# Reordering the hand-over from the mode mix to the output units, and storing the last row block in two halves

## The chip, the cores and the metric

The kernel runs on one core of one Trainium2 chip. The metric is the device time of one execution in microseconds. The profile is one execution taken by the hardware profiler; its span runs from the first to the last instruction of the program.

## What is computed

The input x has 8 batches of 3264 rows of 192 values. The first part is a causal convolution with 7 taps, with softmax weights for each of 8 heads of 24 columns. The second part is a spectral layer on its result:

```
c = conv7(x)                              # (8, 3264, 192)
X = rfft(c, axis=1)[:, :64]               # 64 modes
Y = X * (w_r + 1j*w_i)                    # a 192 x 192 product for each mode
y = irfft(Y, n=3264, axis=1)
u = c + y
out = u + maximum(u @ w_ch, 0)
```

The kernel writes the product as u @ W = c W + G (Y W), where W is w_ch and G is the inverse transform restricted to 64 modes (128 real rows). So each block of output is: c W, plus G times the "second-stage weights" zw = Y W, clamped at zero, plus G times zy = Y, plus c.

## The kernel before

**Work units.** Rows are cut into 27 windows of 122 rows. A unit (h, w, k) is window w for two batches, 4h + 2k and 4h + 2k + 1, as a [128, 384] block in one PSUM bank. There are 108 units; `seq` holds their order, in which the two units k = 0 and 1 of one (h, w) follow each other, so units 0 to 5 are three windows of h = 0, unit 6 is (1, w, 0) and unit 7 is (1, w, 1). `wq` is the list of (h, w).

**What one unit does.**
- c W on TensorE: transposed convolution results (`cTs`) times W, four matmuls of 192 columns (`ab_full` at L546 on the full array).
- z = G zw, one matmul of 384 columns (`gz`, L538), then the clamp on ScalarE (`relu`, L578).
- the y product G zy, one matmul of 384 columns onto the clamped bank (`gy`, L538).
- the add of c on VectorE into the tile t (`finish_unit`, L608); after the second unit of a (h, w) one DMA on SP's queue stores the [128, 4, 192] block (L618).

**Second-stage weights.** `zw_mm(h, k, banks)` makes zw for one pair of batches with four matmuls of 192 columns (L524). With two banks VectorE copies one half (L528) and ScalarE the other (L529); with one bank VectorE copies all 384 columns (L531). Units with k = 0 of h = 0 need zw(0,0), those with k = 1 need zw(0,1); unit 6 needs zw(1,0), unit 7 needs zw(1,1).

**Order.** Engines take their instructions in the order in which the program issues them (`manual_schedule`); there is no scheduler. Before the first zw stands the mode mix in 16 groups (`mix`, L468), whose weights come by DMA. After the last group the result is scaled (`ymix`, L477), transposed (`mix_t`, L503) and copied to `yeT` (VectorE L505, ScalarE L506). While TensorE waits for the mode weights, c W of five units is made ahead (`prefill`), and `keep_warm` issues products of the identity matrix with itself, whose results are not used. Then comes the hand-over that the change edits, and then the steady loop (`for j in range(NF, N + 6)`).

**Steady loop.** It works on half arrays: a product over 128 rows is done as two products over 64 rows each, on row tile 0 and row tile 1, which run beside each other. In step j, the half 0 of z and c W of unit j runs beside half 1 of unit j - 2 (`z_ops`, L556), then the clamp of unit j - 2, then half 0 of the y product of unit j - 4 beside half 1 of unit j - 5 (`y_ops`, L573), and the add of unit j - 5. Two halves write one bank, so the second half waits for a "word": an empty instruction on POOL behind the last product of the first half (L590, in `run_pair`).

**Banks.** There are eight PSUM banks: three in pool `pza`, four in `pt`, one in `py`; `bank(n)` says which pool unit n draws from. A new unit's bank is one whose former unit has been added.

Of the kernel before, what the change touches and what calls it, by code (L numbers as in the profile page):

```python
# [12 lines left out]
F32 = mybir.dt.float32  # L13
BF16 = mybir.dt.bfloat16
# [4 lines left out]
def kernel(  # L19
# [9 lines left out]
    nc = tc.nc  # L29
    B, S, D = x.shape  # L30
# [5 lines left out]
    P = 128  # L36
    WIN = 122
# [50 lines left out]
    ident = constp.tile([P, P], BF16, tag="ident")  # L88
# [66 lines left out]
    for g in range(4):  # L155
        i0 = OV if g == 0 else 0
# [247 lines left out]
    for p in range(4):  # L404
        k = 0
# [88 lines left out]
    def mix_t(g, ymix):  # L494
        zt = mixed[0]
        et = zt[:, 256:512].bitcast(BF16)[:, 0:2 * P].rearrange("p (t k) -> p t k", t=2)
        ets = [et[:, 0, :], et[:, 1, :]]
        q = 16 * (g // 2)
        if g == NGRP - 1:

            ets[1] = zwps[1][:, 0:P // 2].bitcast(BF16)
        for t in range(2):
            nc.tensor.transpose(ets[t], ymix[:, 64 * t:64 * t + P], ident[:])  # L503
        if g == NGRP - 1:
            nc.vector.tensor_copy(out=yeT[:, 0, :, q:q + 16], in_=ets[0].rearrange("p (q b) -> p b q", b=B))  # L505
            nc.scalar.copy(out=yeT[:, 1, :, q:q + 16], in_=ets[1].rearrange("p (q b) -> p b q", b=B))  # L506
        else:
            nc.vector.tensor_copy(out=yeT[:, :, :, q:q + 16],
                                  in_=et.rearrange("p t (q b) -> p t b q", b=B))
# [8 lines left out]
    def zw_mm(h, k, banks):  # L518
        for i in range(2):
            b = 4 * h + 2 * k + i  # L520
            zp = banks[i % len(banks)]
            o = zp[:, D * i:D * i + D] if len(banks) == 1 else zp[:, 0:D]
            for e, wn in ((0, win0), (1, win1)):
                nc.tensor.matmul(o, yeT[:, e, b, :], wn[:, :],  # L524
                                 start=(e == 0), stop=(e == 1), skip_group_check=True)
        zt = zwip.tile([P, 2 * D], BF16, tag=f"zw{h}{k}", name="zw")
        if len(banks) == 2:
            nc.vector.tensor_copy(out=zt[:, 0:D], in_=banks[0][:, 0:D])  # L528
            nc.scalar.copy(out=zt[:, D:2 * D], in_=banks[1][:, 0:D])  # L529
        else:  # L530
            nc.vector.tensor_copy(out=zt[:], in_=banks[0][:, 0:2 * D])  # L531
        b = 4 * h + 2 * k
        zwi[(h, 0, k)] = zt[:]
        zwi[(h, 1, k)] = zy[:, b:b + 2, :].rearrange("p b e -> p (b e)")
# [15 lines left out]
    def z_ops(u, zp, r):  # L550
        h, w, k = u
        lo, hi = 64 * r, 64 * r + 64
        cTp = cTs[2 * h + k]

        def mm(o, lhsT, rhs, start, stop):
            return nc.tensor.matmul(o, lhsT, rhs, start=start, stop=stop, skip_group_check=True,  # L556
                                    tile_position=(lo, 0))

        ops = [lambda: mm(zp[:, 0:2 * D], gst[lo:hi, WIN * w:WIN * w + P], zwi[(h, 0, k)][lo:hi, :],
                          r == 0, False)]  # L560
        for i in range(2):
            c0 = WIN * (NWIN * i + w)
            ops.append(lambda i=i, c0=c0: mm(zp[:, D * i:D * i + D], cTp[lo:hi, c0:c0 + P],
                                             win0[lo:hi, :], False, False))
        c0 = WIN * (2 * NWIN + w)
        ops.append(lambda: mm(zp[:, D * r:D * r + D], cTp[lo:hi, c0:c0 + P],
                              (wB0[0:64, :], win1[64:P, :])[r], False, False))
        return ops

    def y_ops(u, zp, r):  # L570
        h, w, k = u
        lo, hi = 64 * r, 64 * r + 64
        return [lambda: nc.tensor.matmul(zp[:, 0:2 * D], gst[lo:hi, WIN * w:WIN * w + P],  # L573
                                         zwi[(h, 1, k)][lo:hi, :], start=False, stop=(r == 1),
                                         skip_group_check=True, tile_position=(lo, 0))]
# [3 lines left out]

    SYNC = mybir.DependencyInfo(mybir.DependencyClass.Sync, mybir.DependencyReason.DATA)  # L580

    def run_pair(ops0, ops1, behind):


        word = None
        for i in range(max(len(ops0), len(ops1))):
            if i < len(ops0):
                ins = ops0[i]()
                if i == len(ops0) - 1:
                    word = nc.gpsimd.nop()  # L590
                    tc.add_manual_dep(word.ins, ins.ins.name, SYNC, reason="row tile 0 is done")
            if i < len(ops1):
                ins = ops1[i]()
                if i == 0:
                    tc.add_manual_dep(ins.ins, behind.ins.name, SYNC, reason="row tiles on one bank")
        return word

# [3 lines left out]
    def finish_unit(u, zp):  # L603
        h, w, k = u
        if k == 0:
            ts[h] = p3.tile([P, B // 2, D], F32, tag="t", name="t")
        t = ts[h]
        add = nc.vector.tensor_tensor(  # L608
            out=t[:, 2 * k:2 * k + 2, :],
            in0=zp[:, 0:2 * D].rearrange("p (i e) -> p i e", i=2),  # L610
            in1=x_all[:, 4 * h + 2 * k:4 * h + 2 * k + 2, w, :], op=ALU.add)
        if k == 0:
            return
        rows = ((0, 80), (80, LASTVALID)) if w == NWIN - 1 else ((0, P),)
        for r0, r1 in rows:
            dst = bass.AP(tensor=out.tensor, offset=out.offset + (4 * h * S + WIN * w + r0) * D,
                          ap=[[D, r1 - r0], [S * D, B // 2], [1, D]])
            nc.sync.dma_start(out=dst, in_=t[r0:r1, :, :])  # L618


    CH = 7
# [20 lines left out]
    def prefill():  # L642
        zps.append(junk if len(zps) == 2 else bank(len(zps)))
        ab_full(seq[len(zps) - 1], zps[-1])

    def keep_warm(o, n):

        for _ in range(n):
            nc.tensor.matmul(o[:, 0:P], ident[:], ident[:], start=True, stop=True)

    for g in range(NGRP):
        last = g == NGRP - 1
        m = mix(g)
        if g == 6:
            wts0_stack.close()
            cTb = ctx.enter_context(tc.tile_pool(name="stashb", bufs=1)).tile([P, CTW], BF16, tag="cTb")
            nc.vector.memset(cTb[:, NSLOT * WIN:CTW], 0.0)
            cTs[3] = cTb[:, :]
        if g in (0, 1, 2):
            load_weights(g + 7, wp)  # L660
        elif 7 <= g and g + 4 < NGRP:
            load_weights(g + 4, None if g == 10 else wp)
        if not last:
            for _ in range(TPER[g]):
                t_next(2 if g < 6 else 3)
            if gq:
                g_part(gq.pop(0))
            if g == 2:
                load_weights(10, None)

            if g in (10, 11, 14):
                prefill()
            if g == 11:
                junk = bank(2)
        else:
            keep_warm(zwps[0], 4)
        if m is not None:
            mix_t(g, m)
        if g in (12, 13):
            y_back(g - 12)  # L680
        if g in (11, 12, 13):
            keep_warm(junk, 5)
        if g == NGRP - 2:
            zwps += [pt.tile([P, 512], F32, tag="p", name="zwps") for _ in range(2)]
            prefill()
            prefill()
            keep_warm(zwps[0], 6)
# [15 lines left out]
    def gz(n):  # L703
        g_full(seq[n], zps[n], 0)
        relu(zps[n])

    def gy(n):
        g_full(seq[n], zps[n], 1)
        finish_unit(seq[n], zps[n])

    zw_mm(0, 0, zwps[0:2])
    zw_mm(0, 1, zwps[2:3])
    gz(0)
    zw_mm(1, 0, zwps[0:1])
    gz(1)
    gz(2)
    gy(0)
    gz(3)
    gy(1)
    gz(4)  # L720
    zw_mm(1, 1, zwps[1:2])
    gy(2)
    prefill()
    gy(3)
    gz(5)
    N, NF = len(seq), 6
    zword, yword = {}, {}
    for j in range(NF, N + 6):
        o0, o1 = [], []
        if j < N:  # L730
            zps.append(bank(j))
            o0 = z_ops(seq[j], zps[j], 0)
        if NF <= j - 2 < N:
            o1 = z_ops(seq[j - 2], zps[j - 2], 1)
        zword[j] = run_pair(o0, o1, zword.get(j - 2))
        if NF <= j - 2 < N:
            relu(zps[j - 2])
        elif j == NF:
            gy(NF - 2)
            gy(NF - 1)  # L740
        o0, o1 = [], []
        if NF <= j - 4 < N:
            o0 = y_ops(seq[j - 4], zps[j - 4], 0)
        if NF <= j - 5 < N:
            o1 = y_ops(seq[j - 5], zps[j - 5], 1)
        yword[j - 4] = run_pair(o0, o1, yword.get(j - 5))
        if NF <= j - 5 < N:
            finish_unit(seq[j - 5], zps[j - 5])
# [29 lines left out]
```

## Time and profile before

| what | us |
|---|---|
| median of 4 runs | 180.72 |
| lowest and highest run | 179.97 and 182.24 |
| the profiled execution, its own time | 182.24 |
| its span | 180.4 |
| last product of the mode mix starts a burst at | 108.12 |
| first zw product (L524) starts | 109.78 |
| first half product of unit 6 and of unit 7 (L556) | 113.91 and 114.84 |
| last add (L608) ends | 175.35 |

The engine abbreviations are PE for TensorE (PEld its weight loads), DVE for VectorE, ACT for ScalarE, POOL for GpSimd and SP for the engine that issues the stores. A row of the timeline gives the start, the length, the engine, the line, the operation, output and inputs, and how many instructions it covers; a bracket names the idle time before it and what ended that. A matmul's length includes its way through the array, so starts that follow each other closely tell the pace. A row of the windows gives the stretch, its length, the busy time of each engine with the number of instructions, the clock granted to TensorE, the share of the DMA engines and GB/s.

### The profile page before, as it was taken

The page shows a single profiled execution, that of the slowest core. Times are in us where ns is not written, and L with a number is a line of the kernel's source. Part 1 is how long each engine was busy: PE and PEld are TensorE (multiplying, and loading weights), DVE is VectorE, ACT ScalarE, POOL GpSimd, SP SyncE. Part 2 cuts the span into 40 slices and gives each one's busy share as a digit, 9 for nine tenths or more (in the row PEclk, how much of TensorE's full clock was granted, in tenths as well). Part 3 has the DMA queues.
Part 4 walks back from the last instruction along what each step waited for, and adds up shares of the span by engine and source line. Part 5 has one row for each costly group of instructions (what it writes and reads, how often), then busy time and mean ns, then how long its engine had stood idle before and what let it go on. Part 6 is the DMA issues. An engine that isn't in the chain of part 4 may idle for free.

```text
span 180.4 us, 5471 instructions
## 1 busy us (share of the span) xinstructions
PE 147.5 (82%) x2147; PEld 128.8 (71%) x2147; DVE 130.1 (72%) x260; ACT 112.5 (62%) x189; POOL 51.9 (29%) x81
## 2 busy tenths in 40 slices
PE   0377639998898978886877768999999999999960
PEld 0245528877788868775866756799999999999930
DVE  6879985462553446967677524699999999999980
ACT  2358863565656635775766215588888888888840
POOL 7966745549524344441534000000000000000000
PEclk9999996999999999999999999999999999999996
DMA  5999999999999999999999940669999999999995
GB/s 164 178 190 191 192 191 192 191 189 194 190 191 196 202 206 210 204 207 208 205 206 206 208 82 23 213 224 323 353 339 330 370 343 338 358 346 341 313 338 176
DMA packets 65830, 42.02 MB, mean 233 GB/s; under 512 B 29228, under 2 KB 65804, under 8 KB 65804
## 3 DMA queue, kind: packets, MB, share of 16 engines
q0 software_dynamic: 36048, 19.71, 78.7%
q1 hardware_dynamic: 29226, 21.56, 36.0%
q10 hardware_dynamic: 530, 0.39, 0.7%
q8 instruction: 17, 0.28, 0.6%
q14 instruction: 9, 0.07, 0.1%
HBM read 40.19 MB, written 21.01 MB: 339 GB/s over the span
## 4 chain that ended last, share of the span: by engine, by line
PE 55%; DMA 27%; DVE 10%; issue 3%; POOL 2%; ACT 1%; DVEq 0%; POOLq 0%; ACTq 0%
PE z L556 19%; PE z L573 13%; DMA x_all<-in_x_dram 11%; DMA wt<-in_moe_w_i_dram 11%; PE xp L298 7%; PE cp L276 6%; DMA win<-in_moe_w_ch_dram 4%; PE tp L430 3%; DVE x_all L285 3%; PE yp L468 2%; DVE cTa L434 2%; PE tp L310 1%; DVE xs L302 1%; PE z L538 1%; DVE t L608 1%
## 5 line engine op out<-in xcount | busy, mean ns | idle before, releaser
L608 DVE TENSOR_TENSOR t<-z,x_all 128x384 f32<-128x384 f32 x108 | 59.5, 557 | 3.5 <-PE z L573 1.7
L578 ACT ACTIVATE z<-z 128x384 f32<-128x384 f32 x108 | 50.8, 475 | 12.2 <-PE z L556 1.6
L556 PE MATMUL z<-zw,gst 64*128 64x384 bf16 x204 | 46.5, 323 | 0.1
L573 PE MATMUL z<-zy,gst 64*128 64x384 bf16 x204 | 46.2, 323 | 0.2
L556 PE MATMUL z<-win,cTa 64*128 64x192 bf16 x375 | 41.1, 243 | 0.0
L283 ACT CAST x_all<-cp 122x864 bf16<-122x864 f32 (+2 forms) x34 | 28.5, 878 | 16.3 <-PE cp L276 16.3
L556 PEld LDWEIGHTS <-cTa 64*128 64x128 bf16 x450 | 35.1, 94 | 2.8
L276 PE MATMUL cp<-x_all,cband 128*128 128x192 bf16 (+2 forms) x192 | 26.0, 288 | 8.4 <-DVE x_all L285 3.7
L276 PEld LDWEIGHTS <-cband 128*128 128x128 bf16 x192 | 19.6, 109 | 12.4 <-issue 4.7
L285 DVE CAST x_all<-cp 122x768 bf16<-122x768 f32 (+2 forms) x14 | 14.7, 1056 | 13.9 <-PE cp L276 13.5
L61 POOL DMA_DIRECT2D x_all<-in_x_dram x23 | 21.5, 939 | 11.3 <-DMA x_all<-in_x_dram 10.5
L298 PE MATMUL xp<-x_all,fst 122*128 122x192 bf16 (+1 forms) x216 | 22.3, 253 | 0.9 <-DVE x_all L285 0.5
L435 ACT COPY cTa<-tp 128x854 bf16<-128x854 bf16 (+1 forms) x16 | 14.0, 911 | 10.6 <-PE tp L430 10.4
L298 PEld LDWEIGHTS <-fst 122*128 122x128 bf16 (+1 forms) x216 | 18.5, 100 | 2.1 <-DVE x_all L285 0.7
L556 PEld LDWEIGHTS <-gst 64*128 64x128 bf16 x204 | 19.1, 94 | 0.6 <-issue 0.6
L556 PE MATMUL z<-win,cTb 64*128 64x192 bf16 x135 | 19.2, 243 | 0.0
L556 PE MATMUL z<-wB,cTa 64*128 64x192 bf16 x75 | 18.2, 243 | 0.0
L573 PEld LDWEIGHTS <-gst 64*128 64x128 bf16 x204 | 16.2, 93 | 1.0 <-POOLq L590 0.9
L556 PEld LDWEIGHTS <-cTb 64*128 64x128 bf16 x162 | 14.4, 94 | 1.1
L434 DVE COPY cTa<-tp 128x854 bf16<-128x854 bf16 (+1 forms) x17 | 10.6, 621 | 5.4 <-PE tp L430 5.0
L430 PE MATMUL tp<-ident,x_all 122*128 122x122 bf16 x216 | 13.6, 217 | 0.0
L267 POOL DMA_DIRECT2D wt<-in_moe_w_r_dram x14 | 8.6, 613 | 16.7 <-PE yp L468 9.5
(110 smaller groups left out, 176.8 us busy)
## 6 DMA issues: line engine op xcount, KB each, us to landing
out_dram<-t SPq DMA_DIRECT2D x52, 384.0 KB, 3.9
x_all<-in_x_dram POOLq DMA_DIRECT2D x15, 384.0 KB, 11.0
wt<-in_moe_w_r_dram POOLq DMA_DIRECT2D x14, 288.0 KB, 11.0
wt<-in_moe_w_i_dram POOLq DMA_DIRECT2D x14, 288.0 KB, 11.2
x_all<-in_x_dram POOLq DMA_DIRECT2D x7, 480.0 KB, 9.9
fst<-in_moe_w_r_dram POOLq DMA_DIRECT2D x2, 288.0 KB, 10.1
fst<-in_moe_w_i_dram POOLq DMA_DIRECT2D x2, 288.0 KB, 10.7
out_dram<-t SPq DMA_DIRECT2D x2, 240.0 KB, 3.7
```

Of the source, the lines that this page charges most:

```text
L61: nc.gpsimd.dma_start(out=x_all[:, b, c0:c0 + n, :], in_=src)
L276: nc.tensor.matmul(cp[:, j, 0:GRP * n].rearrange("p (w e) -> p w e", w=n), cband[:, h, :], x_all[:, b, w0:w0 + n, GRP * h:GRP * h + GRP], ...
L283: nc.scalar.copy(out=dst, in_=srcv)
L285: nc.vector.tensor_copy(out=dst, in_=srcv)
L298: nc.tensor.matmul(xp[:, 0:D], fst[0:k, c, :], x_all[0:k, b, c, :], start=(u == FIRST[b] and c == w0), stop=(u == LAST[b] and c == w0 + n ...
L430: nc.tensor.transpose(tp[:, WIN * k:WIN * k + WIN], slot_lhsT(p, k0 + k), ident[0:WIN, 0:WIN])
L434: nc.vector.tensor_copy(out=got[0][0], in_=got[0][1])
L435: nc.scalar.copy(out=got[1][0], in_=got[1][1])
L556: return nc.tensor.matmul(o, lhsT, rhs, start=start, stop=stop, skip_group_check=True, tile_position=(lo, 0))
L573: return [lambda: nc.tensor.matmul(zp[:, 0:2 * D], gst[lo:hi, WIN * w:WIN * w + P], zwi[(h, 1, k)][lo:hi, :], start=False, stop=(r == 1), ...
L578: return nc.scalar.activation(out=zp[:, 0:2 * D], in_=zp[:, 0:2 * D], func=ACT.Relu)
L608: add = nc.vector.tensor_tensor(out=t[:, 2 * k:2 * k + 2, :], in0=zp[:, 0:2 * D].rearrange("p (i e) -> p i e", i=2), in1=x_all[:, 4 * h + ...
```

## The change

Five edits, four of them at the hand-over.

1. c W of six units instead of five is made ahead: the third `prefill` in group 14 stands where one bank of `zwps` was reserved, and the `prefill` between the y products is gone. `zwps` now holds one `pt` bank and the `py` bank.
2. The second transpose of the last `mix_t` writes to `zwps[0]`, and `keep_warm` writes to columns 384 to 511 of its bank instead of columns 0 to 127.
3. zw(0,0) is written to the `py` bank and `zwps[0]`; the three later ones use one of these two in turn. The order of z products, clamps and y products becomes 0 2 4 1 3 5 for the clamps, with each zw made when its units need it.
4. The y products of units 3 and 5 are done in halves: half 1 beside half 0 of units 6 and 7, then half 0 alone, which waits for a word of half 1.
5. The last (h, w) of the list stores its first two batches after the unit k = 0 and its last two after k = 1.

```diff
@@ mix_t
-            ets[1] = zwps[1][:, 0:P // 2].bitcast(BF16)
+            ets[1] = zwps[0][:, 0:P // 2].bitcast(BF16)
@@ run_pair
-    def run_pair(ops0, ops1, behind):
-        word = None
+    def run_pair(ops0, ops1, behind1, behind0=None, want=(0,)):
+        words = [None, None]
         for i in range(max(len(ops0), len(ops1))):
...
+            for n, (ops, behind) in enumerate(((ops0, behind0), (ops1, behind1))):
+                if i >= len(ops):
+                    continue
+                ins = ops[i]()
+                if n in want and i == len(ops) - 1:
+                    words[n] = nc.gpsimd.nop()
+                    tc.add_manual_dep(words[n].ins, ins.ins.name, SYNC, reason="the row tile is done")
+                if i == 0 and behind is not None:
                     tc.add_manual_dep(ins.ins, behind.ins.name, SYNC, reason="row tiles on one bank")
-        return word
+        return words[0] if want == (0,) else words
@@ finish_unit
+        split = (h, w) == wq[-1]
-        if k == 0:
+        if k == 0 and not split:
             return
+        i0 = 2 * k if split else 0
+        nb = 2 if split else B // 2
...
-            nc.sync.dma_start(out=dst, in_=t[r0:r1, :, :])
+            nc.sync.dma_start(out=dst, in_=t[r0:r1, i0:i0 + nb, :])
@@ keep_warm
-            nc.tensor.matmul(o[:, 0:P], ident[:], ident[:], start=True, stop=True)
+            nc.tensor.matmul(o[:, 3 * P:4 * P], ident[:], ident[:], start=True, stop=True)
@@ group 14
-            zwps += [pt.tile([P, 512], F32, tag="p", name="zwps") for _ in range(2)]
+            zwps.append(pt.tile([P, 512], F32, tag="p", name="zwps"))
+            prefill()
             prefill()
             prefill()
@@ hand-over
-    zw_mm(0, 0, zwps[0:2])
-    zw_mm(0, 1, zwps[2:3])
+    zy0 = zwps[1]
+    zw_mm(0, 0, [zy0, zwps[0]])
     gz(0)
+    zw_mm(0, 1, [zy0])
+    gz(2)
+    gz(4)
+    gy(0)
     zw_mm(1, 0, zwps[0:1])
     gz(1)
-    gz(2)
-    gy(0)
+    gy(2)
     gz(3)
+    gy(4)
+    zw_mm(1, 1, [zy0])
+    gz(5)
     gy(1)
-    gz(4)
-    zw_mm(1, 1, zwps[1:2])
-    gy(2)
-    prefill()
-    gy(3)
-    gz(5)
@@ loop, steps j = 6 and 7
+        if j - NF < 2:
+            n = (3, 5)[j - NF]
+            o1 = y_ops(seq[n], zps[n], 1)
+            zword[j], word1 = run_pair(o0, o1, None, want=(0, 1))
+            run_pair(y_ops(seq[n], zps[n], 0), [], None, behind0=word1, want=())
+            finish_unit(seq[n], zps[n])
+            continue
         zword[j] = run_pair(o0, o1, zword.get(j - 2))
         if NF <= j - 2 < N:
             relu(zps[j - 2])
-        elif j == NF:
-            gy(NF - 2)
-            gy(NF - 1)
```

More of the change, by code (lines that the diff above doesn't have):

```diff
@@ L580 @@
     SYNC = mybir.DependencyInfo(mybir.DependencyClass.Sync, mybir.DependencyReason.DATA)
-    def run_pair(ops0, ops1, behind):
-        word = None
+    def run_pair(ops0, ops1, behind1, behind0=None, want=(0,)):
+        words = [None, None]
         for i in range(max(len(ops0), len(ops1))):
[L587 to L594, printed above, removed]
+            for n, (ops, behind) in enumerate(((ops0, behind0), (ops1, behind1))):
[6 more added lines that the diff above has]
+                if i == 0 and behind is not None:
                     tc.add_manual_dep(ins.ins, behind.ins.name, SYNC, reason="row tiles on one bank")
-        return word
+        return words[0] if want == (0,) else words
     ts = {}
@@ L605, in finish_unit @@
         if k == 0:
-            ts[h] = p3.tile([P, B // 2, D], F32, tag="t", name="t")
-        t = ts[h]
+            ts[(h, w)] = p3.tile([P, B // 2, D], F32, tag="t", name="t")
+        t = ts[(h, w)]
         add = nc.vector.tensor_tensor(
@@ L611, in finish_unit @@
             in1=x_all[:, 4 * h + 2 * k:4 * h + 2 * k + 2, w, :], op=ALU.add)
-        if k == 0:
+        split = (h, w) == wq[-1]
+        if k == 0 and not split:
             return
+        i0 = 2 * k if split else 0
+        nb = 2 if split else B // 2
         rows = ((0, 80), (80, LASTVALID)) if w == NWIN - 1 else ((0, P),)
         for r0, r1 in rows:
-            dst = bass.AP(tensor=out.tensor, offset=out.offset + (4 * h * S + WIN * w + r0) * D,
-                          ap=[[D, r1 - r0], [S * D, B // 2], [1, D]])
-            nc.sync.dma_start(out=dst, in_=t[r0:r1, :, :])
+            dst = bass.AP(tensor=out.tensor, offset=out.offset + ((4 * h + i0) * S + WIN * w + r0) * D,
+                          ap=[[D, r1 - r0], [S * D, nb], [1, D]])
+            nc.sync.dma_start(out=dst, in_=t[r0:r1, i0:i0 + nb, :])
     CH = 7
```

## The prediction

> **What bounds the kernel now.** I read the busy table, then the chain of waits around the edited code, then the queues of VectorE and of the stores.
>
> ```profile
> PE 147.5 (82%) x2147; PEld 128.8 (71%) x2147; DVE 130.1 (72%) x260; ACT 112.5 (62%) x189; POOL 51.9 (29%) x81
> ...
> PEclk9999996999999999999999999999999999999996
> ...
> L608 DVE TENSOR_TENSOR t<-z,x_all 128x384 f32<-128x384 f32 x108 | 59.5, 557 | 3.5 <-PE z L573 1.7
> ```
>
> The table alone decides nothing. From 117 to 172 us the chain of waits is TensorE only (L556 and L573), a step every 0.572 us, one step per unit; the add at L608 follows each step with a gap of about 15 ns. An add lasts 557 ns, but where adds queue up they start 465 to 475 ns apart, so VectorE is not the bound there, nor ScalarE (clamps start 371 ns apart when queued). The change leaves the steady steps as they are. It can move only two things: when they begin (before: 115.27 us, row tile 0 of unit 8), and what comes after the last add (175.35 us). So the sum has two terms.
>
> The chain of waits through the start (start, length, what):
>
> ```profile
> 109.43 0.30 DVE yeT L505
> 109.73 0.05 issue
> 109.78 0.52 PE zwps L524 x4
> 110.30 0.02 issue
> 110.32 0.33 ACT zw L529
> 110.65 0.04 issue
> 110.69 0.32 PE z L538
> ...
> 112.63 0.33 PE zwps L524 x4
> 112.96 0.16 PE z L538
> 113.12 0.13 PE z L546 x2
> 113.25 0.06 issue
> 113.31 0.56 DVE zw L531
> 113.87 0.04 issue
> 113.91 0.57 PE z L556 x4
> ```
>
> It shows that the start is latency, not TensorE work: copy of yeT, four products for zw, copy, clamp, and at 113.31 the last copy of a zw on VectorE, for which unit 6 waits.
>
> **The change, part by part.** The prices come from the timeline: matmul starts lie 56, 82 and 162 ns apart for 128, 192 and 384 columns; the result is out 219, 246 and 322 ns after the start; PE to VectorE or ScalarE takes 0.04 us more, back to PE 0.05.
>
> *Unit 5's c W ahead.* Four matmuls of L546 (0.33 us, 112.96 to 113.29) leave the start and stand at 106.9, before the wait for the last mode weights, which ends at 108.12; TensorE idles 0.92 us there, so they cost nothing. Gain in TensorE work: 0.33 us, worth time only if TensorE is what is late. The ident products on cols 384:512 of other banks cost nothing.
>
> *Bank of the second transpose.* It now shares bank zwps[0] with the four ident products behind it. In the built order the first of these waits for ScalarE's copy L506. That copy ended at 109.68, so they start at 109.74 instead of 109.22, and the first zw product at 109.74 + 4 x 0.056 = 109.96 instead of 109.78: **+0.18**. The ident matmuls compute nothing needed; they only stand ahead in TensorE's queue.
>
> *Order 0 2 4 1 3 5, zw over two banks.* From 109.96, zw(0,0) goes to two banks and ScalarE's half ends at 110.81, so clamp 0's product starts at 110.86 (before 110.69). Now zw(0,1) runs behind it (111.02 to 111.52), then units 2 and 4. y product 0 needs clamp 0 (111.22 to 111.70): 111.76, before 111.58. zw(1,0) runs 111.92 to 112.41, then z of 1, y of 2, z of 3, y of 4, zw(1,1) 112.90 to 113.39, z of 5, y of 1, to 113.55. No clamp is late in this order: those of 2, 4, 1, 3 are ready 0.05 us or more before their y products.
>
> What is late next is VectorE, which takes adds and zw copies in program order:
>
> ```profile
> 110.65 0.56 DVE L531 CAST zw<-zwps 128x384 bf16<-128x384 f32 x1
> 111.38 0.56 DVE L531 CAST zw<-zwps 128x384 bf16<-128x384 f32 x1 [0.17 <-PE zwps L524]
> 112.38 1.02 DVE L608 TENSOR_TENSOR t<-z,x_all 128x384 f32<-128x384 f32 x2 [0.44 <-PE z L538]
> 113.31 0.55 DVE L531 CAST zw<-zwps 128x384 bf16<-128x384 f32 x1
> 113.78 2.03 DVE L608 TENSOR_TENSOR t<-z,x_all 128x384 f32<-128x384 f32 x4
> ```
>
> Before: three zw copies, two adds, the copy of zw(1,1), four adds. After: zw(0,1) at 111.55, add 0 at 112.18, zw(1,0) at 112.65, adds 2 and 4 at 113.11 and 113.58, and only then **zw(1,1) at 114.04, done 114.60** (before 113.31 and 113.86). Behind it: unit 7's first product, with everything on TensorE queued after that.
>
> *Units 6 and 7 with y halves.* Unit 6 starts at 113.65 (113.55, plus 0.10 for the change from full array to half array, as between unit 5's y product at 114.585 + 0.162 and 114.844); before 113.91. Half 1 of unit 3's y runs beside it, free. Half 0 waits for the word through POOL: in the drain such halves start 0.43 us apart, so 114.1. TensorE then stands until 114.65 for zw(1,1); unit 7 starts there, before 114.84. Half 0 of unit 5's y follows 0.46 us later (word, LDWEIGHTS), 0.16 us long, and unit 8 can start at 114.65 + 0.62 = **115.27**. Before it was 115.27. **Net of the start: 0.0 us.** The 0.33 us taken off TensorE turns into a wait for VectorE.
>
> *One unseen cost.* In the profile add 0 starts at 112.38 though its last wait ended at 111.96: 0.42 us with no cause in the trace. If that start-up belongs to the first add, all of VectorE behind it slides to the copy of zw(1,1) at 114.40 and unit 8 begins 0.36 us later. [...] Below: without the +0.18 and with no POOL delay, -0.3.
>
> *Last row block in two halves.* The half for k=0 is issued at about 174.9 instead of 175.38. One more DMA issue (0.37 us on SP) fits before the second half at 175.38; nothing queues behind it. Whether it helps is read from the stores:
>
> ```profile
> 174.00:175.00 1.00, 0.44 (x3) 0.09 (x1) 1.00 (x3) 0.00 (x0) 0.00 (x0) 1.00 0.96 320
> 175.00:176.00 1.00, 0.00 (x0) 0.00 (x0) 0.35 (x1) 0.00 (x0) 0.00 (x0) 1.00 1.09 371
> 176.00:177.00 1.00, 0.00 (x0) 0.00 (x0) 0.00 (x0) 0.00 (x0) 0.00 (x0) 1.00 1.10 371
> ```
>
> The last column is GB/s. The last four adds start 0.47 us apart, two per 384 KB store, so the last three stores are issued 0.93 to 0.98 us apart; one takes 1.06 us at 371 GB/s. From 174.8 to 177.8 the 16 engines have no hole, and one engine runs on to 179.1 alone with its backlog. [...] By the row they are full, and bytes that arrive earlier only join a queue: 0.0. I take the row. Bounds: -0.5 and +0.1.
>
> **Sum.** 0.0 (start) + 0.0 (end) against the profiled execution: 182.24 us stays 182.2 (span 180.4 stays 180.4). That was the slowest of the four runs; on their median of 180.72 the same sum gives **180.7**.
>
> **The rivals.**
> *VectorE late by its first add.* +0.36, 181.1. For it: the 0.42 us stood before exactly this instruction. Against: no other add shows it.
> *The half store pays and the start gains a little.* -0.5, 180.2. For it: the end is pure DMA from 175.4 on. Against: 371 GB/s without a hole.
> *The clock drops (slower).*
>
> ```profile
> 23.40:26.90 3.50, 1.02 (x10) 0.99 1.60 191
> 26.90:30.30 3.40, 3.40 (x22) 0.51 1.60 191
> ...
> 105.30:108.80 3.50, 2.58 (x46) 1.00 0.15 28
> 108.80:112.20 3.40, 2.90 (x27) 1.00 0.08 20
> ```
>
> A stretch with TensorE 1.02 us busy was followed by 3.4 us at clock 0.51. The change opens holes: 109.4 to 109.7, 110.3 to 110.9, 114.2 to 114.65. If they brought a stretch down to that share, 3.41 us at half speed would cost 1.7 us in the TensorE-bound part: 182.4. It decides from roughly a third busy (1.02 of 3.5 dropped it, 2.17 of 3.4 at 101.9 to 105.3 did not); the holes take 0.9 us from 2.9, so it should hold.
> *The halves don't overlap as written.* If half 1 of each y product ran alone, 0.16 us for unit 5 only: 180.9.
>
> **How the numbers follow.** Chances: no change 0.58, first add late 0.18, half store pays 0.15, clock 0.06, no overlap 0.03. About 1% (1.8 us) is what a measurement of this kernel tells from no change; only the clock case reaches near it, and the runs themselves lie 2.3 us apart. So faster 0.04, same 0.90, slower 0.06. The range: costs from -0.6 to +0.5 us, and as much again for the median of a few such runs: 179.6 to 181.8.
>
> **What would show it.** The first ident product behind the last transposes starts only after L506 ends (or my +0.18 is wrong); zw(1,1)'s copy starts near 114.0 and unit 7's first product directly behind it; add 0 within 0.1 us of its wait; unit 8 near 115.3 (with the stretch before it shifted alike); the DMA near 370 GB/s until about 2.5 us after the last add, with the last store's landing unmoved relative to the last add. The prediction is wrong if unit 8 begins over 0.5 us earlier, if the DMA has holes behind 175, or if the granted clock drops between 109 and 119.

## The result, and the profile after

The changed kernel takes 181.06 us in the median (43 runs), the kernel before 180.87 us (64 runs). The ratio is **1.0014, 95% interval 0.9997 to 1.0031**: no difference that this measurement can tell, as predicted. The ratio is of fast runs alone, without two of the 43 that lay over 1.5% above the fastest, so it isn't the quotient of the medians. The same kernel was measured again later, as one of the experiments, and gave 1.0044 [1.0023, 1.0064], a small slowdown that is clear of its interval; the middle of the two is 1.003, or +0.5 us. The forecast of "no change" held, but not every zero in its sum was a zero.

From the page of the changed kernel, its busy table, the granted clock in 40 slices, and the group of the adds:

```profile
PE 146.9 (81%) x2149; PEld 128.5 (71%) x2149; DVE 129.3 (72%) x260; ACT 112.9 (63%) x189; POOL 51.8 (29%) x81
...
PEclk9999789999999999999999996999999999999996
...
L608 DVE TENSOR_TENSOR t<-z,x_all 128x384 f32<-128x384 f32 x108 | 59.7, 557 | 3.5 <-PE z L573 1.4
```

Totals and adds are nearly as before. The clock row is not: the single 6 in the middle of the span is a slice around 110 us, in the hand-over, where the kernel before had a 9.

Both profiled spans are 180.4 us (own times 182.34 and 182.24), which hides three differences. The table gives the distances between four landmarks; the last add is in both kernels the 101st after unit 6's.

| stretch, us | before | after |
|---|---|---|
| span's start to the start of the last mode-mix product | 108.35 | 106.42 |
| from there to the start of unit 6's add | 9.11 | 10.37 |
| from there to the start of the last add | 57.34 | 57.35 |
| last add's end to the span's end | 5.00 | 5.75 |

The first row depends on when the mode weights arrive; in the 14 profiles of this study it lies between 106.35 and 108.35, also among kernels whose code up to there is the same. So two profiles are compared from the last mode-mix product on, and not by their spans. On that measure the profiled execution lost 1.26 us in the hand-over and 0.75 us at the end.

**The hand-over.** The chain of waits of the changed kernel (start, length, what):

```profile
108.19 0.34 PE zwps L524 x4
108.53 0.02 issue
108.55 0.33 ACT zw L529
108.88 0.04 issue
108.92 0.32 PE z L538
109.25 0.62 PE zwps L524 x4
109.87 0.96 PE z L538 x3
```

Four zw products take 0.34 us at 108.19 and the next four, of the same shape, 0.62 us at 109.25. Where the same hand-over ran at the full clock (the experiment "The hand-over alone" below), both groups took 0.34 us. The windows of the same profile, PE to POOL busy with numbers of instructions, then the granted clock:

```profile
105.70:109.10 3.40, 1.98 (x28) 1.38 (x29) 0.65 (x2) 0.92 (x3) 0.14 (x1) 1.00 0.08 21
109.10:112.50 3.40, 3.40 (x16) 2.14 (x15) 2.03 (x4) 1.84 (x5) 0.00 (x0) 0.50 0.08 19
112.50:115.90 3.40, 3.40 (x45) 2.57 (x45) 2.72 (x6) 1.58 (x4) 0.00 (x0) 0.99 0.19 66
```

The granted clock was 0.50 from 109.1 to 112.5. This is the slower rival of the prediction, in this execution, and one of the signs by which the prediction said it would be wrong. Whether it is the rule is a question for the experiments. The profiled execution was a long one: 182.34 us against the median of 181.06.

**The end.** The issues of the last block's two halves on SP's queue, after:

```profile
174.63 0.53 SPq L621 DMA_DIRECT2D out_dram<-t  x1
...
175.21 0.76 SPq L621 DMA_DIRECT2D out_dram<-t  x1
```

The last add ended at 174.68. The second half was issued 0.53 us later, because SP was still at work on the first. Before, the one store was issued at 175.38, 0.03 us after the last add's end:

```profile
175.38 0.37 SPq L618 DMA_DIRECT2D out_dram<-t  x1
```

### The profile page after: what moved, and what is told of

The parts are those of the page before. It is cut to its first block, busy times and chain, and to the rows that moved or that the text cites. A ratio compares the mean times of both kernels' runs of the same rounds, so it can differ in the third digit from the quotient of the medians.

```text
span 180.4 us, 5477 instructions
## 1 busy us (share of the span) xinstructions
PE 146.9 (81%) x2149; PEld 128.5 (71%) x2149; DVE 129.3 (72%) x260; ACT 112.9 (63%) x189; POOL 51.8 (29%) x81
## 4 chain that ended last, share of the span: by engine, by line
DMA 50%; PE 37%; POOL 7%; issue 2%; DVE 1%; ACT 1%; DVEq 0%; POOLq 0%; ACTq 0%
DMA x_all<-in_x_dram 26%; DMA wt<-in_moe_w_i_dram 24%; PE z L556 19%; PE z L573 14%; POOL x_all L61 4%; PE z L538 2%; PE zwps L524 1%; PE yp L468 1%; DVE t L608 1%; POOL wt L267 1%; POOL x_all L74 1%; POOL x_all L67 0%; POOL x_all L66 0%; DVEq L782 0%; POOL midx L123 0%
## 5 line engine op out<-in xcount | busy, mean ns | idle before, releaser
L573 PE MATMUL z<-zy,gst 64*128 64x384 bf16 x208 | 47.2, 323 | 0.2
L276 PE MATMUL cp<-x_all,cband 128*128 128x192 bf16 (+2 forms) x192 | 25.0, 281 | 7.8 <-DVE x_all L328 5.0
L298 PE MATMUL xp<-x_all,fst 122*128 122x192 bf16 (+1 forms) x216 | 21.4, 246 | 0.9 <-DVE x_all L285 0.5
L298 PEld LDWEIGHTS <-fst 122*128 122x128 bf16 (+1 forms) x216 | 17.7, 98 | 1.9 <-DVE x_all L285 0.7
```

The costliest lines, as they stand in the source:

```text
L276: nc.tensor.matmul(cp[:, j, 0:GRP * n].rearrange("p (w e) -> p w e", w=n), cband[:, h, :], x_all[:, b, w0:w0 + n, GRP * h:GRP * h + GRP], ...
L298: nc.tensor.matmul(xp[:, 0:D], fst[0:k, c, :], x_all[0:k, b, c, :], start=(u == FIRST[b] and c == w0), stop=(u == LAST[b] and c == w0 + n ...
```

## The experiments

Four questions: what does the start cost at full clock; is it VectorE's queue that takes the gain; how often does the clock drop; what does the half store cost? The runs fall into three groups: the first four kernels below, the next four, the last four. Each group has its own runs of the kernel before (medians 180.73, 180.48 and 180.59 us). Stage times are from one profile each; "start" is from the last mode-mix product to unit 6's add (9.11 before), "end" from the last add's end to the span's end (5.00 before). In all kernels the steady part between takes 57.34 or 57.35 us.

### The half store alone

The kernel before, with only the `split` lines of `finish_unit`.

```diff
 # kernel before
+        split = (h, w) == wq[-1]
...
-            nc.sync.dma_start(out=dst, in_=t[r0:r1, :, :])
+            nc.sync.dma_start(out=dst, in_=t[r0:r1, i0:i0 + nb, :])
```

> The kernel before with the store of the last row block in two halves, and nothing else. Theory 1 (the DMA engines have no hole at the end, bytes that arrive earlier only join a queue): 0.0 us, ratio 0.999 to 1.001, time from the end of the last add to the last landing as before, 4.1 us. Theory 2 (the half store pays, as if the engines were idle): -0.5 us, 3.6 us from last add to last landing. Theory 3 (the store before it keeps SP busy, so that the last one is issued late): +0.3 us, the last store is issued 0.3 to 0.5 us behind the end of the last add instead of 0.03.

Measured: 1.0029 [1.0011, 1.0046]; start 9.10, end 5.81. The half store by itself costs about 0.5 us, all of it behind the last add. The last landing comes 4.46 us after the last add's end (4.07 before), and from the landing to the span's end there are 1.35 us instead of 0.93. The second half was issued 0.56 us after the last add's end (the one store before: 0.03), later than even the third theory had it. The second difference is the surprise, and has an experiment of its own below.

### The hand-over alone

```diff
-        split = (h, w) == wq[-1]
+        split = False
```

> The changed kernel with the last row block stored whole, as before. Theory 1 (the two halves are worth nothing): the same as the changed kernel within 0.1 us. Theory 3 (the second half is issued late because SP still issues the first): 0.3 us less than the changed kernel, last add to last landing 4.1 instead of 4.4 us.

Measured: 1.0000 [0.9979, 1.0021]; start 9.12, end 5.35. This profile had the full clock through the hand-over, so the prediction's times can be read in it. VectorE's timeline:

```profile
110.81 0.56 DVE L531 CAST zw<-zwps 128x384 bf16<-128x384 f32 x1 [0.87 <-PE zwps L524]
111.42 0.56 DVE L608 TENSOR_TENSOR t<-z,x_all 128x384 f32<-128x384 f32 x1
111.91 0.56 DVE L531 CAST zw<-zwps 128x384 bf16<-128x384 f32 x1
112.38 1.01 DVE L608 TENSOR_TENSOR t<-z,x_all 128x384 f32<-128x384 f32 x2
113.31 0.55 DVE L531 CAST zw<-zwps 128x384 bf16<-128x384 f32 x1
```

The order is the predicted one: zw(0,1), add, zw(1,0), two adds, zw(1,1). The last copy starts 5.69 us after the last mode-mix product (107.62). The chain of waits goes from ScalarE's copy L506 through the ident products (L652) and later through this last copy to unit 7's first product at 113.91:

```profile
108.68 0.28 ACT yeT L506
108.96 0.04 issue
109.00 0.38 PE zwps L652 x4
109.38 0.34 PE zwps L524 x4
...
112.46 0.93 DVE t L608 x2
113.39 0.47 DVE zw L531
113.87 0.04 issue
113.91 0.32 PE z L556
```

The end did not behave as the third theory said: with the block stored whole and issued 0.03 us after the last add, the last landing still came 4.42 us after that add, as late as in the changed kernel's profile (4.40). One landing in one profile says little about what a store costs.

### Without the four ident products behind the transposes

```diff
-    keep_warm(zwps[0], 4)
```

> The changed kernel without the four ident products behind the last two transposes. Theory 1 (the wait for the copy L506 ahead of them costs 0.18 us on the chain): first zw product 0.06 us behind the end of the copy L505 instead of 0.23, -0.18 us. Rival (they keep the clock up, and their loss costs more): more executions with a stretch of half clock between 105 and 119 us, mean granted clock lower, +0.3 us or more.

Measured: 1.0024 [1.0001, 1.0047]; start 8.95, end 5.47. The first zw product now starts 0.06 us after the end of copy L505, as before the change, instead of 0.23. The start is 0.17 us shorter than in the experiment above: the ident wait is real, sits on the path, and has the predicted size (0.18). In the median it can't be seen: 0.17 us is 0.1%, less than the interval is wide. The rival, that without these products the clock drops more often, is not settled: this profile had the full clock in the hand-over, while 8 of the 18 runs took over 181.5 us, against 16 of 43 in the changed kernel.

### zw(1,1) made early

```diff
     gz(1)
+    zw_mm(1, 1, [zy0])
     gy(2)
...
-    zw_mm(1, 1, [zy0])
     gz(5)
```

> The changed kernel with zw(1,1) made right behind the z product of unit 1, so that VectorE copies it ahead of the adds of units 2 and 4. Theory 1 (the start is held by VectorE's queue, where this copy stood behind two adds): at the full clock unit 7 starts directly behind half 0 of unit 3's y and unit 8 about 0.4 us earlier, counted from the last product of the mode mix; -0.4 us against the changed kernel. Rival (the clock gate decides, the queue doesn't matter): no difference in the median, and the stretch from the mix to unit 8 is 6.9 us at the full clock and over 8 us where the clock was dropped, in this kernel as in the changed one.

Measured: 1.007 [1.0043, 1.0097] from only 9 runs; start 8.86, end 5.22. Time and stages disagree: neither start nor end is longer than in the changed kernel. Only the wait for the mode weights was (107.94 us to the last mode-mix product, 106.42 there), which lies anywhere from 106.35 to 108.35 in the 14 profiles, and the profiled execution, 181.69 us, was among the faster ones. It was measured again unchanged (below).

### Early zw(1,1), one store

The edit above and `split = False`.

> The changed kernel with zw(1,1) made early and the last block stored whole. If the slow median of the kernel with zw(1,1) early comes from its end (half stores), this one is 0.3 us faster than the kernel before. If it comes from the clock gate in the hand-over (the emptier stretch falls under the threshold more often), this one stays over 1 us above the kernel before in most executions, although its stretch from the mix to the first steady add is 8.86 us or less at the full clock; an execution with a half-clock stretch between 105 and 116 us would show it.

Measured: 0.9975 [0.995, 1.0000], median 179.92 us; start 8.86, end 4.85. VectorE's timeline, with the two copies now together and the adds of the start behind them:

```profile
110.69 1.01 DVE L531 CAST zw<-zwps 128x384 bf16<-128x384 f32 x2
111.62 2.41 DVE L608 TENSOR_TENSOR t<-z,x_all 128x384 f32<-128x384 f32 x5
```

The copy of zw(1,1) moves from 5.69 to 4.75 us after the last mode-mix product, and the start gets 0.26 us shorter. So VectorE's queue did hold up the new order. Of the 0.94 us by which the copy comes earlier only 0.26 arrives: from the first z product on, the chain of waits is then TensorE's own work, as in the chain shown further below.

### The same with more ident products before the mode mix

```diff
-            keep_warm(zwps[0], 6)
+            keep_warm(zwps[0], 14)
```

> As the kernel with zw(1,1) early and the block stored whole, but with 14 instead of 6 ident products in the wait for the last mode weights (8 more, 0.45 us of a hole of 0.57 us or more). Clock theory: the stretch around the hand-over is fuller, the share of executions above 181.5 us falls to that of the kernel before or below, and the median is 0.5 us or more under that kernel's. Queue theory alone: no change, or +0.1 us where the weights come early.

Measured: 0.9969 [0.9947, 0.9991]; start 8.86, end 4.59. Eight more products in TensorE's wait for the last mode weights cost nothing. In this profile, as in the one without them, the clock stayed up in the hand-over; whether they keep it up can't be told from that. The 0.5 us that the clock theory expected from them did not come: the medians are 179.87 and 179.92 us, and 1 and 2 of 22 runs took over 181.5 us.

### The ident products moved ahead of the mode mix

The four behind the transposes removed, 16 instead of 6 before the mix, early zw(1,1), one store.

```diff
-            keep_warm(zwps[0], 6)
+            keep_warm(zwps[0], 16)
...
-    keep_warm(zwps[0], 4)
```

> As the kernel with zw(1,1) early and the block stored whole, with the four ident products behind the last transposes taken out and ten more in the wait for the last mode weights (16 instead of 6). At the full clock the first zw product follows the copy L505 by 0.06 us and the stretch from the mix to the first steady add is 8.7 us (8.86 less 0.18): 0.4 us faster than the kernel before if the clock holds. Clock theory: it holds about as well as in the kernel with 14; if the products are needed just where they stood, the share of executions above 181.5 us is higher.

Measured: **0.9965 [0.9942, 0.9988]**, median 179.89 us; start 8.69, end 4.68. This is 0.35% faster than the kernel before, clear of the interval, and below both results of the changed kernel (1.0014 and 1.0044, from other groups of runs). Its start is 0.42 us shorter than before, and the two parts add up: 0.25 for the early copy and 0.17 for the idents. In time it can't be told from the two versions above (0.9975 and 0.9969). Its chain of waits holds only TensorE from the first z product on:

```profile
107.42 0.30 DVE yeT L505
107.73 0.05 issue
107.78 0.52 PE zwps L524 x4
...
108.69 0.32 PE z L538
109.01 0.33 PE zwps L524 x4
109.34 0.56 PE z L538 x3
109.89 0.33 PE zwps L524 x4
```

### One more DMA in the kernel before

One small DMA long before the end is issued in two parts; the stores are untouched. That shifts which of the eight semaphores of SP's DMAs the last store uses, from the last to the first, as the half store does.

```diff
 # kernel before, the copies to zy
+            if i == YPE:
+                nc.sync.dma_start(out=zy[16 * i:16 * i + 8, :, :], in_=ymix[0:64, :])
+                nc.sync.dma_start(out=zy[16 * i + 8:16 * i + 16, :, :], in_=ymix[64:128, :])
```

> The kernel before with one of its two small copies of mode-mix results into zy issued as two DMAs, so that one more DMA stands on SP's queue and the last store signals the first of the eight DMA semaphores instead of the eighth; the stores themselves are unchanged. Theory A (SP's closing waits run over the semaphores in order, so when the last landing signals the first one, seven waits of 0.06 us come after it): from the last landing to the end 1.35 us instead of 0.93, +0.4 us, ratio about 1.002. Theory B (what the split costs lies in the issue and the transfer of the half stores): nothing changes, ratio 0.999 to 1.001.

Measured: 1.0014 [0.9987, 1.0041]; start 9.12, end 5.46. The landing is where it was (4.10 us after the last add's end), and from it to the span's end there are 1.35 us, as in the half-store kernels. What happens there is in SP's closing waits. The semaphore instructions at the program's end, in the last stretch of the kernel before, of the changed kernel and of this one (duration in ns, then first and last start). The last landings came at 179.43, 179.08 and 177.51 us:

```profile
L773 SPq EVENT_SEMAPHORE  x1: 28/28/28, 179.4 to 179.4; - x1
```

```profile
L782 SPq EVENT_SEMAPHORE  x8: 28/28/28, 179.1 to 179.5; - x8
```

```profile
L777 SPq EVENT_SEMAPHORE  x8: 28/28/28, 177.5 to 178.0; - x8
```

SP waits for the eight semaphores one after the other. When the last store is on the last of them, the other seven waits are over by the time it lands and one instruction remains. When it is on the first, all eight remain, 0.06 us apart: 7 x 0.06 = 0.42 us. The profile shows this plainly; the timed interval holds both 0 and 0.42 us (0.23%), so it doesn't confirm it.

### The changed kernel with the order of the waits restored

One of the copies into x_all is issued by POOL instead of SP, so that the last store is on the last semaphore again.

```diff
-        nc.sync.dma_start(out=x_all[WIN:P, :, w, :], in_=x_all[0:OV, :, w + 1, :])
+        (nc.gpsimd if w == 20 else nc.sync).dma_start(out=x_all[WIN:P, :, w, :], in_=x_all[0:OV, :, w + 1, :])
```

> The changed kernel with one of the three small copies inside x_all (window 20) issued from POOL instead of SP, so that one DMA fewer stands on the hardware queues and the second half store signals the eighth DMA semaphore, the last one that SP waits for at the end. Theory A (the order of the closing waits): from the last landing to the end 0.93 us instead of 1.35, -0.4 us against the changed kernel; what is left of the split's cost is the late issue of the second half. Theory B (issue and transfer alone): no change against the changed kernel.

Measured: 1.0011 [0.9993, 1.0029]; start 9.12, end 4.99. The changed kernel itself, in the same group of runs, gave 1.0044 (next experiment), so this is some 0.6 us less where 0.4 was expected; the two intervals overlap a little. Landing to span's end is 0.92 us again, with two halves still stored. One closing wait remains after the landing:

```profile
L782 SPq EVENT_SEMAPHORE  x1: 28/28/28, 177.7 to 177.7; - x1
```

So the profiles show the 0.42 us move with the semaphore's place in both directions. The second half was still issued late here, 0.34 us after the last add's end. This was also a second profile of the changed hand-over at full clock, with the start at 9.12.

### The changed kernel again

No edit.

> The changed kernel itself once more, for a second profile. At the full clock the stretch from the last product of the mode mix to the first steady add should be 9.1 us, as in the changed kernel with the block stored whole; where the clock is halved in it, 10.4 us as in the first profile. From the last landing to the end 1.35 us either way. Time 0.2 to 0.4 us above the kernel before.

Measured: 1.0044 [1.0023, 1.0064]; start 10.30, end 5.89. The time is 0.8 us above the kernel before, more than the 0.2 to 0.4 expected; the stages are as expected for a dropped clock. The granted clock dropped in the hand-over again. The profiled execution, 182.78 us, was the longest of the 22. The windows:

```profile
105.80:109.20 3.40, 2.02 (x30) 1.23 (x28) 0.65 (x2) 0.87 (x3) 0.14 (x1) 1.00 0.09 20
109.20:112.60 3.40, 3.30 (x15) 2.24 (x16) 1.59 (x3) 1.61 (x5) 0.00 (x0) 0.50 0.09 21
```

This stretch began 1.0 us before the last mode-mix product. Two stretches that lie alike were not followed by a drop. First the kernel with only the half store, which has the order of before; its stretch began 1.0 us before that product too:

```profile
105.40:108.80 3.40, 2.21 (x31) 1.61 (x32) 0.74 (x3) 0.92 (x3) 0.14 (x1) 1.00 0.09 22
108.80:112.20 3.40, 3.21 (x24) 2.08 (x24) 2.81 (x6) 2.38 (x6) 0.00 (x0) 1.00 0.10 24
```

Then the kernel with early zw(1,1) and one store, which up to there has the order of the changed kernel; its stretch began 0.65 us before the product, that of the changed kernel's first profile 0.70:

```profile
105.80:109.20 3.40, 2.09 (x29) 1.48 (x30) 0.65 (x2) 0.92 (x3) 0.14 (x1) 1.00 0.06 15
109.20:112.60 3.40, 3.40 (x30) 2.15 (x28) 2.94 (x7) 2.67 (x6) 0.00 (x0) 1.00 0.10 24
```

TensorE was busy 1.98 and 2.02 us in the stretches before a drop, 2.09 and 2.21 us in those before none. These windows are rounded to 0.1 us; with the edges of the clock's own record, 3.41 us apart, the changed kernel's two profiles have 2.01 and 2.03 us (from 105.72 and 105.79 on), early zw(1,1) with one store 2.06 (from 105.76) and the half store alone 2.21 (from 105.39). So a drop and none lie 0.03 us apart. The 3.41 us stretches have no fixed place against the work: in the 14 profiles their edges lie differently against the last mode-mix product (one lies 0.70 us before it in the changed kernel; in the kernel before, counted on from the drop that began at 26.85 us, about 3.0 us before it). The four rows fit one reading: a drop takes an order with little work behind the transposes, and a stretch that happens to cover both the wait for the mode weights and those holes. By it the changed order has the smaller margin (2.02 against 2.21 us at the same place, one profile each), though 2.09 us in that order were followed by no drop. This is a reading and not shown; no run changed the work in that stretch alone. How many executions drop is open: both profiles of the changed kernel did, the two others with the same hand-over did not, and the timings alone don't tell. The two that dropped lay 1.3 and 1.5 us above the medians of their kernels, about what a drop cost, so they may be the exception.

### Early zw(1,1) with the half store, again

No edit against its first measurement.

> The changed kernel with zw(1,1) made early, once more: its first measurement (1.3 us above the kernel before, 9 executions) agrees neither with its own profile nor with the same kernel with the block stored whole. Theory 1 (its start is 0.26 us shorter, its end 0.4 to 0.8 us longer): 0.1 to 0.5 us above the kernel before. Rival (this start together with the half stores falls into a slower mode): again over 1 us above it.

Measured: 1.0018 [1.0001, 1.0035]; start 8.85, end 5.98. The 1.007 of the first time did not come back; its cause is open. Against the same kernel with one store (0.9975, in another group of runs) the half store costs some 0.4% here, again behind the last add.

### Everything together, with the half store

The idents moved, early zw(1,1), the order of the waits restored, and the half store.

> The fastest start so far (zw(1,1) early, ident products moved into the wait for the last mode weights) with the last block in two halves and the second half on the eighth DMA semaphore. Theory 1 (the DMA engines are full at the end): no faster than the same start with the block stored whole, whose median was 179.9 us and ratio 0.9965; 0.0 to +0.3 us against it. Theory 2 (the split was a gain that the order of the closing waits hid): -0.3 us against it, ratio 0.995.

Measured: 0.9995 [0.9973, 1.0018]; start 8.87, end 4.80. It is not resolved from the kernel before. The second half was issued 0.16 us after the last add's end and landed 3.87 us after it, against 0.03 and 3.75 with one store: no gain from the half store is to be seen, even with the waits in order. The 0.3 us of gain that the second theory expected did not come: against the version with one store (0.9965, in another group) this is 0.3% more, with intervals that overlap. The start is 0.18 us longer than in the version with one store, whose order on TensorE and VectorE is the same. The chain of waits has a gap in it at the first y product:

```profile
109.73 0.33 PE z L538 x2
110.06 0.08 issue
110.14 0.32 PE z L538
```

That product needs the row block of zy that a DMA writes from the scaled mode result. The last part of it landed 3.26 us after the last mode-mix product here, 2.99 in the version with one store, and the product started at 3.40 and 3.22; its weight load began 0.11 us after the landing in both. So the first y product has a second input that can be late, which no step of the prediction had.

## Why the prediction was right, and where it was not

**The start, net 0.0: right.** Measured from the last mode-mix product, the prediction's times and those of the hand-over alone are:

| step | predicted | measured |
|---|---|---|
| first zw product | 1.61 | 1.60 |
| copy of zw(0,1) | 3.20 | 3.19 |
| add 0 | 3.83 | 3.80 |
| copy of zw(1,0) | 4.30 | 4.29 |
| adds of units 2 and 4 | 4.76, 5.23 | 4.76, 5.23 |
| copy of zw(1,1) | 5.69 | 5.69 |
| unit 6's first half product | 5.30 | 5.28 |
| unit 7's first half product | 6.30 | 6.29 |
| unit 8's first half product | 6.92 | 6.93 |

The add of unit 6, and with it the steady part, starts at 9.12 against 9.11. The step "0.33 us off TensorE turns into a wait for VectorE" is shown, not only consistent: with the copy moved ahead of the adds 0.26 us come back, with the idents moved as well 0.42. One thing the prediction leaves out: before the change unit 6 waited for the copy of zw(1,1) although it doesn't use it. By the code it takes the PSUM bank in which zw(1,1) was made, and the copy is the last to read it.

**The ident wait, +0.18: right.** 0.17, and taking it away returns 0.17.

**Add 0's start-up, taken as 0.0: the number right, its reason not shown.** In the hand-over alone add 0 starts 0.05 us after the copy before it (110.81 + 0.56, then 111.42), with no hole. The 0.42 us did not belong to the add, but they are no accident of one profile either: all three profiles with the former order have them (0.40 to 0.42 us). Their cause is open. No run shows a reason for the 0.0, which stood as the author's estimate; what the runs show is 0.05 us in the changed order and 0.40 to 0.42 us in the former.

**The end, 0.0 with +0.1 as its upper bound: the failed step.** The half store costs +0.5 us (1.0029 alone, 1.0011 to 1.0046). The reasoning about the transfers was near: from 175 to 177 us the DMA moved 369 GB/s, and the half stores gained nothing. No run shows the lower bound of -0.5: in its place stand the +0.5 us of the half store alone. In the changed kernel's windows at the end:

```profile
174.00:175.00 1.00, 0.00 (x0) 0.00 (x0) 0.68 (x2) 0.00 (x0) 0.00 (x0) 1.00 0.66 222
175.00:176.00 1.00, 0.00 (x0) 0.00 (x0) 0.00 (x0) 0.00 (x0) 0.00 (x0) 1.00 1.09 369
176.00:177.00 1.00, 0.00 (x0) 0.00 (x0) 0.00 (x0) 0.00 (x0) 0.00 (x0) 1.00 1.09 369
```

Two terms were wrong or missing. The first is SP's time at an issue. The step "one more DMA issue (0.37 us on SP) fits before the second half" failed: the 0.37 us were those of the one 384 KB store, and the 16 halves of the eight half-store profiles took 0.53 to 0.87 us each. So the second half was issued 0.16 to 0.60 us after the last add's end, not 0.03. In the changed kernel an earlier store had held SP up as well:

```profile
172.79 1.16 SPq L621 DMA_DIRECT2D out_dram<-t  x1
```

That one made the first half late (0.05 us before the last add's end) and the second with it. Why an issue takes longer is not shown: full DMA engines alone are not the reason, since the one store of the kernel before took 0.37 us beside 371 GB/s.

The second term is the order of the closing waits, 0.42 us, in no row that the prediction showed. How the rest of the 0.5 us comes about is not settled: the average landing of the eight half-store profiles is 4.25 us after the last add, that of the six others 3.99, and each group scatters by over 0.7.

**The clock: the estimate too low.** The drop and its place were named, and the rival got a chance of 0.06. "Roughly a third busy" was the author's estimate from the two stretches that the prediction names, one with TensorE 1.02 us busy (a drop followed) and one with 2.17 (none followed); it took the low end and so saw a wide margin. No run shows that limit: here 1.98 and 2.02 us of 3.40 were followed by a drop. The holes were counted from the stretch that lay there in one profile, though the next execution may lay its stretches differently. The price per drop was 1.26 and 1.19 us in the two profiles; the prediction said 1.7. Whether 0.06 was too small a chance for the median is not shown, since both profiled executions were long ones.

**The total.** 180.7 was predicted and 181.06 came. At full clock the start is 0.0; the end is about +0.5; the drops add some more in a part of the executions. The two results (+0.25 and +0.8 us) stand on both sides of that. Two of the signs that the prediction set itself went against it: the last landing moved (4.40 us after the last add, 4.07 before; but 4.42 with the block stored whole), and the granted clock dropped between 109 and 119 us. For the start "no change" was right for its reasons, but for the 0.0 of add 0, for which no run shows one. For the whole it held because half a microsecond, 0.3%, is within what the forecast called no change; that part is luck.

## What to carry to other kernels

Taking work off the engine that looks busy gained nothing here, because another engine's program order set the first moment of the steady loop. In such a case list that engine's instructions in order, find the late one that others wait for, and move it ahead of those that nobody waits for yet. One line moved gave back 0.26 us that 0.33 us of removed matmuls had not. Splitting the last store brought nothing with the DMA engines at 369 GB/s. Before splitting one, count the time of its issues on the queue, and what the program still waits for after the landing.

## What was not expected of the hardware

- The place of the last DMA's semaphore in the closing order is worth up to 0.42 us: 0.92 to 0.93 or 1.34 to 1.35 us from the last landing to the span's end, and nothing between, in all 14 profiles.
- Issuing a 384 KB store took SP between 0.37 and 1.32 us (median 0.37), a 192 KB half 0.53 to 0.87 us, in the 14 profiles.
- The busy share alone does not say when the clock drops. In the hand-over 2.02 us of 3.40 were followed by a drop and 2.09 were not, yet earlier in the changed kernel a stretch with less went by without one:

```profile
78.40:81.80 3.40, 1.94 (x41) 1.88 (x39) 3.21 (x8) 2.54 (x4) 1.22 (x3) 1.00 1.21 206
81.80:85.20 3.40, 3.25 (x69) 2.85 (x67) 1.50 (x4) 1.70 (x3) 1.22 (x2) 1.00 1.21 207
```

It had 41 matmuls instead of 28 to 30. In two other profiles (the hand-over alone, and early zw(1,1) again) the clock dropped once more, at 68.6 us, after a stretch with TensorE 1.98 us busy in 32 matmuls. What exactly is counted stays open.
